# Attention layers: maxima stored by way of a 32x32 block transpose, outputs combined on GpSimd inside attention, loads of a pair head by head

## The chip, the cores and the metric

The kernel runs on one core of one Trainium2 chip. The metric is the device time of one execution in microseconds (us), the median of several runs. Five engines run side by side, each through its own queue in order: TensorE (PE, with its weight loads PEld), VectorE (DVE), ScalarE (ACT), GpSimd (POOL) and SyncE (SP). SP issues all the DMAs of this kernel; an instruction that waits on SP holds back every DMA queued behind it. TensorE's clock is granted by a throttle, and the profile tells its share of full speed.

## The reference

Four layers in a row, A, B, A, B. Each normalizes its input, attends and adds the result to what came in. A is multi-head attention with 32 heads of 18 elements; B has 32 query heads and one shared key and value head.

```python
B, S, D, H = 1, 2048, 576, 32          # Dh = D // H = 18
def _A_ref(x, wqkv, wo):
    qkv = (x @ wqkv).reshape(B, S, 3, H, Dh).transpose(2, 0, 3, 1, 4)
    q, k, v = qkv[0], qkv[1], qkv[2]
    scores = jnp.einsum("bhqd,bhkd->bhqk", q, k) * (Dh ** -0.5)
    p = softmax(scores, axis=-1)
    o = jnp.einsum("bhqk,bhkd->bhqd", p, v)
    return o.transpose(0, 2, 1, 3).reshape(B, S, D) @ wo
# _B_ref: q as above from x @ wq; k = x @ wk and v = x @ wv are one head for all 32
x = A_x
x = x + _A_ref(layernorm(x), A_wqkv, A_wo)
x = x + _B_ref(layernorm(x), B_wq, B_wk, B_wv, B_wo)
x = x + _A_ref(layernorm(x), A_wqkv, A_wo)
x = x + _B_ref(layernorm(x), B_wq, B_wk, B_wv, B_wo)
```

All is float32. Layernorm has no weights.

## The kernel before

A layer has three stages: projection, attention, output projection. They overlap at their ends.

**Projection.** Tokens go in eight tiles of 256. Rows are normalized, transposed and split into a high part (rounded to the float32r type of the matrix unit) and a low part (the rest), and multiplied in three products (high by high, high by low, low by high: `TERMS`). The results, split again, are stored to DRAM in `qk_d`; the values stay in `vbuf`.

**Attention.** Heads go in 16 pairs p; a pair's queries go in four parts u of 512. Each (p, u), called a unit here, is eight steps (`STEPS`), so a layer has 64 units and 512 steps (`ns`). The rows of a pair's queries and keys lie in two of six slots of the tile `big`, the first head on partitions 0 to 63, the second on 64 to 127. They are loaded from `qk_d` by `load_pair` (L410), four loads of 54 rows x 2048 in A (query and key of two heads), two in B (the key is shared and loaded once); each load is 432 KB.

In every step PE does four score matmuls to find the maxima (`max_mm`, L432, DVE reduces each 1024 columns at L438), four score matmuls for the exponential (`exp_mm`, L549, ACT takes the exponential at L552 into `pt`), and the products of `pt` with the values (`pv_block`, L566) into the bank `oacc`. The maxima run `LEAD` = 14 steps ahead of the exponentials: after a unit's last maximum, `max_final` reduces on DVE (L527, `mm`), negates and splits on POOL (L529 to L532, `hl`), `max_store` (L536) writes the 128 x 16 values to `m_d` in DRAM, transposing them element by element on the way, and `max_rows` (L540) loads them back as two further rows of the queries in `big`, two DMAs, one for each head. The key has ones there, so that the second score matmul subtracts the maximum. `exp_mm` of the unit cannot begin before these rows are in `big`.

A unit's output in `oacc` (128 x 512) has, for each of the two heads, two partial sums at partitions 64a and 64a + 32: 18 rows of outputs and one of the softmax's sum. ACT copies it to SBUF (L572, `oc`). Then, each at its step after the unit's end: `o_out` issues four loads that spread the sums over partitions (`lt`, L586) and four stores of the outputs (L590) to `o_d[0]` and `o_d[1]`; `l_sum` adds the two sums on POOL (L594); `l_inv` inverts on DVE (L598); `l_out` stores the inverses to `r_d` (L601); `l_spread` copies them, repeated over 18 rows, from DRAM to DRAM into `o_d[2]` (L607). The order of all this is written out by hand: `at(step, function)` puts a function into the list of a step, and each step runs its list and then its matmuls. So the order on every queue follows the step numbers, while each engine goes on as soon as what it waits for is there. The constants `NM_AT`, `ROW_AT`, `O_AT` and so on are those steps.

The weights of the output projection and of the next layer are loaded and split into high and low on POOL during attention (`load_w`, L121 and L143).

**Output projection.** For each of eight token tiles of 256, `out_rows` (L235, L237) loads three tensors: the two partial outputs and the inverses. `out_t` adds the partial outputs (POOL, L244 and L248), multiplies by the inverses (DVE, L245 and L249) and splits into high (ACT, L119, or DVE, L121) and low (DVE, L247 and L251). `out_w` (L258) multiplies each chunk of 128 tokens in two halves with the weights (`natural`, L198), adds the residual rows (L263) and stores them (L264). The next layer's first rows are loaded and normalized meanwhile.

Of the kernel before, what the change touches and what calls it, by code (L numbers as in the profile page):

```python
# [38 lines left out]

STEPS = 8
LEAD = 14
NM_AT = 2
ROW_AT = 4
O_AT = 4
SUM_AT = 7
INV_AT = 9
R_AT = 10
SPREAD_AT = 12  # L50


FIRST_A = 6
# [2 lines left out]
AHEAD_B = 3  # L56

OUT_AHEAD = 2  # L60
TAIL = 2


@with_exitstack
def tile_kernel(ctx: ExitStack, tc: tile.TileContext, A_x, A_wqkv, A_wo, B_x, B_wq, B_wk, B_wv, B_wo, out):
# [31 lines left out]


    m_d = [dram.tile([2, 2, 4, P], F32, name=f"m_d{i}") for i in range(4)]
    o_d = dram.tile([3, D, S], F32, name="o_d")  # L100
    r_d = dram.tile([H, S], F32, name="r_d")
    x_d = [dram.tile([S, D], F32, name=f"x_d{i}") for i in range(2)]


# [12 lines left out]
    def copy(eng, dst, src):  # L117
        if eng is nc.scalar:
            eng.activation(dst, src, AF.Copy)  # L119
        else:  # L120
            eng.tensor_scalar(dst, src, 1.0, 0.0, op0=OP.mult, op1=OP.add)  # L121
# [107 lines left out]

    def out_rows(tt):  # L230
        ts = slice(tt * 256, tt * 256 + 256)
        o4 = [pool.tile([P, 4, 256], F32, tag="o4", bufs=4, name="o4") for _ in range(3)]
        o1 = pool.tile([P, 3, 256], F32, tag="o1", bufs=2, name="o1")
        for i in range(3):
            nc.sync.dma_start(o4[i], o_d[i, :512, ts].rearrange("(c p) t -> p c t", p=P))  # L235
        for r in (0, 64):
            nc.sync.dma_start(o1[r:r + 64], o_d[:, 512:, ts].rearrange("i p t -> p i t"))  # L237
        ors[tt] = o4, o1

    def out_t(tt, hi):  # L240
        (a, b, r), l = ors.pop(tt)
        ot = ots_[tt] = pool.tile([P, 9, 256], F32R, tag="xt", name="ot")
        ot_f = ot.bitcast(F32)
        nc.gpsimd.tensor_tensor(a, a, b, op=OP.add)  # L244
        nc.vector.tensor_tensor(a, a, r, op=OP.mult)  # L245
        copy(hi, ot[:, 0:4], a)
        nc.vector.tensor_tensor(ot[:, 5:9], a, ot_f[:, 0:4], op=OP.subtract)  # L247
        nc.gpsimd.tensor_tensor(l[:, 0], l[:, 0], l[:, 1], op=OP.add)  # L248
        nc.vector.tensor_tensor(l[:, 0], l[:, 0], l[:, 2], op=OP.mult)  # L249
        copy(hi, ot[:, 4], l[:, 0])  # L250
        nc.vector.tensor_tensor(ot[64:, 4], l[64:, 0], ot_f[64:, 4], op=OP.subtract)  # L251
# [6 lines left out]
    def out_w(c, x_new_prev):  # L258
        xr = xrs.pop(c)
        ot = ots_[c // 2][:, :, c % 2 * P:(c % 2 + 1) * P]  # L260
        for h in range(2):
            cs = slice(h * 288, (h + 1) * 288)
            nc.vector.tensor_tensor(xr[:, cs], natural(ot, h, mtile), xr[:, cs], op=OP.add)  # L263
        nc.sync.dma_start(x_new_prev[c * P:(c + 1) * P, :], xr)  # L264

    ors, ots_, lts, rls = {}, {}, {}, {}
    xhs, xts = {}, {}

    def trans(c):
        tt, u = divmod(c, 2)  # L270
        if u == 0:
            xts[tt] = pool.tile([P, 9, 256], F32R, tag="xt", name="xt")
        xh = xhs.pop(c)
        split_rows(xts[tt][:, :, u * P:(u + 1) * P], *transposed(xh, xh[:, 512:640]))

# [12 lines left out]

    def out_proj(x_res_prev, x_new_prev):

        for c in range(3):
            load_res(c, x_res_prev)
        yield -1
        for c in range(NCH):
            out_w(c, x_new_prev)
            load_res(c + 3, x_res_prev)
            if c >= OUT_AHEAD:
                run_tail(TAIL)
            tt = c // 2
            if c % 2 == 0 and 1 <= tt < 7:  # L300
                out_t(tt + 1, nc.scalar)
            if c % 2 == 1 and tt < 6:
                out_rows(tt + 2)
            yield c
        assert not tail and not ors


    load_x(0, x_in)
    for layer in range(4):
# [83 lines left out]
        def load_rows(slot, c0, step, t0, t1):  # L393

            for a in range(2):
                c = c0 + a * step
                nc.sync.dma_start(big_f[64 * a:64 * a + 3 * DH, slot, t0:t1],
                                  qk_d[c:c + DH, :, t0:t1].rearrange("c i t -> (c i) t"))
# [8 lines left out]
                fixed_rows(q_slot(p), False)  # L407
            load_rows(q_slot(p), 2 * p * DH, DH, t0, t1)

        def load_pair(p):  # L410
            load_q(p)
            if is_a:
                load_k(p)

        mxs, nms, pts, ocs = {}, {}, {}, {}

# [108 lines left out]
        def max_final(p, u):  # L525
            mm = pool.tile([P, 8], F32, name="mm")
            nc.vector.reduce_max(mm, mxs.pop((p, u)), axis=AX.X)  # L527
            neg = pool.tile([P, 8], F32, name="neg")
            nc.gpsimd.tensor_scalar(neg, mm, -1.0, 0.0, op0=OP.mult, op1=OP.add)  # L529
            hl = pool.tile([P, 2, 8], F32R, name="hl")  # L530
            copy(nc.gpsimd, hl[:, 0], neg)
            nc.gpsimd.tensor_tensor(hl[:, 1], neg, hl.bitcast(F32)[:, 0], op=OP.subtract)  # L532
            nms[p, u] = hl.bitcast(F32)

        def max_store(p, u):
            nc.sync.dma_start(m_d[u].rearrange("j a q p -> p (j a q)"), nms.pop((p, u)).rearrange("p j b -> p (j b)"))  # L536

        def max_rows(p, u):
            for a in range(2):
# [37 lines left out]
            if 0 <= n < ns and (half or n % STEPS):  # L577
                pv_block(n, half if n % STEPS else None)

        def o_out(p, u):  # L580
            oc = ocs.pop((p, u))
            lt = lts[p, u] = pool.tile([P, 2, 8], F32, name="lt")
            for a in range(2):
                for i in range(2):
                    r = 64 * a + 32 * i + DH
                    nc.sync.dma_start(lt[64 * a:64 * a + 64, i, :], oc[r:r + 1, :])  # L586
            for a in range(2):
                for i in range(2):
                    r, c = 64 * a + 32 * i, (2 * p + a) * DH
                    nc.sync.dma_start(o_d[i, c:c + DH, u * 512:(u + 1) * 512], oc[r:r + DH, :])  # L590

        def l_sum(p, u):
            lt = lts[p, u]
            nc.gpsimd.tensor_tensor(lt[:, 0], lt[:, 0], lt[:, 1], op=OP.add)  # L594

        def l_inv(p, u):
            rl = rls[p, u] = pool.tile([P, 8], F32, name="rl")
            nc.vector.reciprocal(rl, lts.pop((p, u))[:, 0])  # L598

        def l_out(p, u):  # L600
            nc.sync.dma_start(r_d[2 * p:2 * p + 2, u * 512:(u + 1) * 512].rearrange("a (t e) -> a t e", e=8),  # L601
                              rls.pop((p, u)))

        def l_spread(p, u):
            us = slice(u * 512, (u + 1) * 512)
            for h in (2 * p, 2 * p + 1):
                nc.sync.dma_start(o_d[2, h * DH:(h + 1) * DH, us], r_d[h:h + 1, us].to_broadcast([DH, 512]))  # L607

        todo = {}

# [4 lines left out]
        for p in range(NPAIR):  # L615
            for u in range(4):
                b = STEPS * (4 * p + u) + STEPS - 1
                at(b + NM_AT, max_store, p, u)
                at(b + ROW_AT, max_rows, p, u)
                for d, f in ((O_AT, o_out), (SUM_AT, l_sum), (INV_AT, l_inv), (R_AT, l_out), (SPREAD_AT, l_spread)):  # L620
                    at(b + LEAD + d, f, p, u)
            if p + 1 < NPAIR:
                b = LEAD + 32 * (p - 2) + 32
                at(b if p >= 2 else max(b, LEAD + 2 + 16 * p), load_pair, p + 1)
        for c in range(5):
            at(49 + 4 * c, finish_loads)
            at(48 + 4 * c, load_wsm, c, A_wo if is_a else B_wo, nc.gpsimd, nc.gpsimd, True)
# [6 lines left out]
                at(b + 2, load, c, (0,), nc.gpsimd, nc.gpsimd, True)  # L634

        b = LEAD + ns
        at(b - 10, out_rows, 0)
        at(b - 7, out_t, 0, nc.vector)
        at(b - 6, out_rows, 1)
        at(b - 3, out_t, 1, nc.vector)  # L640
# [4 lines left out]
        for st in range(done // 4, ns + LEAD + O_AT + 1):  # L645
            se = st - LEAD
            for f, args in todo.pop(st, []):
                f(*args)
            for i in range(4):
                if 0 <= se < ns:  # L650
                    exp_mm(*divmod(se // STEPS, 4), se % STEPS * 4 + i, st >= ns)
                if done < st * 4 + i + 1 <= ns * 4:
                    max_mm(*divmod(st // STEPS, 4), st % STEPS * 4 + i)
                left = 2 * -se - i // 2
                if i == 1:
                    pv_slot(se - 2, 1)
                elif i == 3:
                    pv_slot(se - 1, 0)
                if se < 0 and i % 2 and len(fill) * every >= left and (left % every == 0 or len(fill) >= left):
                    f, args = fill.pop(0)  # L660
                    f(*args)
            if se == ns - 1:
                tail = [todo.pop(n, []) for n in range(ns + LEAD + O_AT + 1, ns + LEAD + SPREAD_AT)]
# [37 lines left out]
```

## Time and profile before

| | us |
|---|---|
| median of 3 runs | 7502.77 (7489.41 to 7513.87) |
| the profiled execution's own time | 7491.71 |
| its span, first to last instruction | 7489.9 |
| PE busy | 6380.8 (85%) |
| DVE busy | 5458.4 (73%) |
| ACT busy | 4720.5 (63%) |
| POOL busy | 521.3 (7%) |

The mean granted clock is 0.912. A profile line of the waits reads: who waited, for what, how many us in all, how many times, the longest. A line of the groups reads: line, engine, operation, what is written and read, shapes, count; then busy us, the mean of one in ns; then the idle time of the engine just before, and what ended it. A timeline line reads: start in us, duration, engine, line, operation, how many in a row. SPq is SP's queue issuing a DMA; its duration is that of the issue, not of the transfer.

### The profile page before, as it was taken

Reading aid. Unit: us, or ns where it says so; the run is one execution under the profiler, and the core shown is the slowest. Engines: PE = TensorE matmul, PEld = TensorE weight load, DVE = VectorE, ACT = ScalarE, POOL = GpSimd, SP = SyncE. Lnnn points to the kernel's source line nnn. Section 1 sums busy time; section 2 is a strip of 40 time slices with the busy share of each in tenths; the row PEclk is TensorE's granted clock in tenths of the full one; section 3 lists DMA queues with packets and bytes.
Section 4 is the critical chain, followed back from the end, with each engine's and each line's share of the span. In section 5 each row is a group of like instructions: output and inputs, shape, how many; then the busy total and the mean of one; then the engine's idle time right before and its main releaser. Section 6 shows DMA issues by size and latency. Waiting matters only on the chain.

```text
span 7489.9 us, 132853 instructions
## 1 busy us (share of the span) xinstructions
PE 6380.8 (85%) x53280; PEld 2788.6 (37%) x53280; DVE 5458.4 (73%) x5480; ACT 4720.5 (63%) x8896; POOL 521.3 (7%) x1479
## 2 busy tenths in 40 slices
PE   9888888888788888889698888888887888888897
PEld 9332222233633333333493322222336333333334
DVE  3787777776478888888337877777864788888883
ACT  2576766676157777777325767666761577777773
POOL 1000000001100000000210000000011000000001
PEclk9899989899889999999898999998998899999998
DMA  5311111112621111111552111111125211111104
GB/s 183 70 35 22 29 29 30 30 21 52 196 48 25 21 21 21 21 21 21 151 163 68 36 21 30 29 30 30 22 60 188 48 25 21 21 21 21 21 12 141
DMA packets 910355, 385.49 MB, mean 51 GB/s; under 512 B 679865, under 2 KB 845041, under 8 KB 900017
## 3 DMA queue, kind: packets, MB, share of 16 engines
q1 hardware_dynamic: 909736, 377.01, 21.6%
q8 instruction: 418, 6.85, 0.4%
q14 instruction: 201, 1.64, 0.1%
HBM read 226.22 MB, written 164.46 MB: 52 GB/s over the span
## 4 chain that ended last, share of the span: by engine, by line
DMA 42%; PE 31%; SPq 11%; ACT 7%; issue 5%; DVE 3%; POOL 1%; ACTq 0%; POOLq 0%; DVEq 0%
DMA m_d<-hl 31%; PE pse L549 13%; PE oacc L566 10%; SPq L586 6%; DMA big<-m_d 5%; ACT pt L552 5%; SPq L590 4%; PE psq L327 4%; PE psn L198 2%; DMA o<-o_d 2%; PE psm L432 2%; ACT oc L572 2%; DMA r_d<-rl 1%; DVE mx L438 1%; POOL o L244 1%
## 5 line engine op out<-in xcount | busy, mean ns | idle before, releaser
L438 DVE TENSOR_REDUCE mx<-psm 128x1 f32<-128x1024 f32 x4096 | 4980.2, 1223 | 1254.1 <-PE psm L432 1064.6
L552 ACT ACTIVATE pt<-pse 128x512 f32<-128x512 f32 x8192 | 4415.9, 600 | 1740.8 <-PE psm L432 1233.9
L549 PE MATMUL pse<-big 64*128 64x512 f32 x8192 | 3180.5, 467 | 812.6 <-DMA big<-m_d 703.6
L432 PE MATMUL psm<-big 62*128 62x512 f32 x8192 | 3228.5, 472 | 52.5 <-DVE mx L438 42.7
L566 PE MATMUL oacc<-pt,vbuf 128*19 128x256 f32 (+1 forms) x30720 | 2653.0, 419 | 0.0
L549 PEld LDWEIGHTS pse<-big 64*128 64x128 f32 x8192 | 1305.2, 195 | 2818.3 <-ACT pt L552 1937.6
L432 PEld LDWEIGHTS psm<-big 62*128 62x128 f32 x8192 | 1301.1, 196 | 155.6 <-DVE mx L438 131.7
L566 PEld LDWEIGHTS oacc<-pt,vbuf 128*19 128x19 f32 x30720 | 529.8, 98 | 1451.3 <-issue 1445.2
L198 PE MATMUL psn<-wsm,ot 128*128 128x288 f32 x1792 | 296.9, 335 | 203.4 <-DVE xr L263 203.4
L327 PE MATMUL psq<-xt,big 128*128 128x256 f32 (+1 forms) x3136 | 422.0, 295 | 25.3 <-DVE ev L337 16.2
L327 PEld LDWEIGHTS psq<-xt,big 128*128 128x128 f32 (+1 forms) x3136 | 402.5, 198 | 41.6 <-DVE ev L337 19.2
L529 POOL TENSOR_SCALAR neg<-mm 128x8 f32<-128x8 f32 x256 | 50.4, 197 | 4834.8 <-DVE mm L527 4728.4
L198 PEld LDWEIGHTS psn<-wsm,ot 128*128 128x128 f32 x1792 | 289.7, 226 | 211.7 <-issue 210.0
L331 ACT ACTIVATE ev<-psq 128x512 fp32r<-128x512 f32 (+2 forms) x148 | 73.1, 494 | 434.7 <-PE psq L327 409.6
L119 ACT ACTIVATE ot<-o 128x1024 fp32r<-128x1024 f32 (+1 forms) x48 | 35.3, 736 | 402.3 <-DVE o L245 362.7
L337 DVE TENSOR_TENSOR ev<-psq,ev 128x512 fp32r<-128x512 f32 (+2 forms) x120 | 69.7, 592 | 197.6 <-ACT ev L331 187.2
L245 DVE TENSOR_TENSOR o<-o,o 128x1024 f32<-128x1024 f32 x32 | 42.2, 1320 | 222.9 <-POOL o L244 114.4
L263 DVE TENSOR_TENSOR xr<-psn,xr 128x288 f32<-128x288 f32 x128 | 56.3, 455 | 183.8 <-PE psn L198 183.0
L572 ACT ACTIVATE oc<-oacc 128x512 f32<-128x512 f32 x256 | 154.5, 604 | 34.9 <-PE oacc L566 34.3
L198 PE MATMUL psn<-wsm,xt 128*128 128x288 f32 x896 | 125.0, 295 | 0.0
L198 PEld LDWEIGHTS psn<-wsm,xt 128*128 128x128 f32 x896 | 120.1, 188 | 2.9 <-issue 1.5
L594 POOL TENSOR_TENSOR lt<-lt 128x8 f32<-128x8 f32 x256 | 53.0, 207 | 822.9 <-DMA lt<-oc 822.3
(52 smaller groups left out, 1004.5 us busy)
## 6 DMA issues: line engine op xcount, KB each, us to landing
big<-qk_d SPq DMA_DIRECT2D x180, 432.0 KB
qk_d<-ev SPq DMA_DIRECT2D x192, 256.0 KB
o<-o_d SPq DMA_DIRECT2D x96, 512.0 KB
o_d<-oc SPq DMA_DIRECT2D x1024, 36.0 KB
qk_d<-ev SPq DMA_DIRECT2D x240, 128.0 KB
o_d<-r_d SPq DMA_DIRECT2D x512, 36.0 KB
lt<-oc SPq DMA_DIRECT2D x1024, 2.0 KB
x_d<-xr SPq DMA_DIRECT2D x48, 288.0 KB
```

The lines of the kernel that those rows point to most:

```text
L198: nc.tensor.matmul(ps, lhs[:, xc, :], wsm[:, wc, h * 288:(h + 1) * 288], start=i == 0, stop=i == len(TERMS) - 1)
L244: nc.gpsimd.tensor_tensor(a, a, b, op=OP.add)
L327: nc.tensor.matmul(ps[:n, k, :], w[:, wc, :n], xt[:, xc, :], start=j == 0, stop=j == len(TERMS) - 1)
L331: nc.scalar.activation(ev[0][:n, :g], ps[:n, :g], AF.Copy)
L432: nc.tensor.matmul(ps[:, i % 2], q[b:b + KM, c0:c0 + P], k[b:b + KM, kb * 512:(kb + 1) * 512], start=True, stop=True)
L438: nc.vector.reduce_max(mxs[p, u][:, a * 4 + qc, j // 8:j // 8 + 1], ps.rearrange("p a t -> p (a t)"), axis=AX.X)
L549: nc.tensor.matmul(e, k[r:r + KE, kc * P:(kc + 1) * P], q[r:r + KE, u * 512:(u + 1) * 512], start=True, stop=True)
L552: nc.scalar.activation(pt, e, AF.Exp, scale=SCALE)
L566: nc.tensor.matmul(oacc[j:j + DH + 1, cs], v[:, kc, 2 * p + a if is_a else 0, :], pts[p, u, i][:, cs], start=kc < 2, stop=kc >= 14 and hal ...
L572: nc.scalar.activation(oc, oacc, AF.Copy)
L586: nc.sync.dma_start(lt[64 * a:64 * a + 64, i, :], oc[r:r + 1, :])
L590: nc.sync.dma_start(o_d[i, c:c + DH, u * 512:(u + 1) * 512], oc[r:r + DH, :])
```

## The change

Four things change together.

- **The maxima's store.** `hl` is one of two fixed tiles of 128 x 32, filled with zeros once at the start. `max_store` transposes it on DVE by blocks of 32 x 32 and issues four stores, one for each block of 32 partitions, each of 16 rows of 32 elements. `max_rows` stands one step later (`ROW_AT` 5 for 4).
- **The outputs.** `o_sum` copies the second partial of each head to the partitions of the first and adds, on POOL; so the two sums are added in the same step as the outputs. `l_part` spreads the two sums with two loads; `l_inv` and `l_out` are as before; `l_rows` loads the inverses, repeated over 18 rows, into SBUF (`rbs`); `o_mul` multiplies and splits on POOL; `o_out` stores the high and low part, four DMAs.
- **The output projection** loads the high and low part as they are; `out_t` is gone. Three buffers of `xt` instead of two hold them. The store of a chunk is issued after the work of the next, and a residual load two chunks ahead instead of three.
- **The pair's loads** are issued one by one, one every eight steps (every four for the second pair), instead of all in one step.

```diff
-ROW_AT = 4
-O_AT = 4
-SUM_AT = 7
-INV_AT = 9
-R_AT = 10
-SPREAD_AT = 12
+ROW_AT = 5
+SUM_AT = 3
+L_AT = 4
+INV_AT = 7
+R_AT = 7
+RB_AT = 9
+MUL_AT = 11
+O_AT = 13
...
+    rbs = [cst.tile([P, 512], F32, name=f"rb{i}") for i in range(2)]
+    sums = [cst.tile([P, 512], F32, name=f"os{i}") for i in range(2)]
+    hls = [cst.tile([P, 32], F32R, name=f"hl{i}") for i in range(2)]
+    for t in rbs + sums + [h_.bitcast(F32) for h_ in hls]:
+        nc.gpsimd.memset(t, 0.0)
...
     def out_rows(tt):
...
+        for i in range(2):
+            nc.sync.dma_start(ot[:, 5 * i:5 * i + 4], o_d[i, :512, ts].rearrange("(c p) t -> p c t", p=P))
+            nc.sync.dma_start(ot[64 * i:64 * i + 64, 4], o_d[i, 512:, ts])
-    def out_t(tt, hi):
...
+        def load_part(p, i):
+            if i < 2:
+                if i == 0 and p < 3:
+                    fixed_rows(q_slot(p), False)
+                load_rows(q_slot(p), 2 * p * DH, DH, 0, S, (i,))
+            else:
+                if i == 2 and p < 3:
+                    fixed_rows(k_slot(p), True)
+                load_rows(k_slot(p), D + 2 * p * DH, DH, 0, S, (i - 2,))
...
         def max_store(p, u):
-            nc.sync.dma_start(m_d[u].rearrange("j a q p -> p (j a q)"), nms.pop((p, u)).rearrange("p j b -> p (j b)"))
+            tr = pool.tile([P, 32], F32, name="tr")
+            nc.vector.transpose(tr, nms.pop((p, u)).bitcast(F32))
+            for b in range(4):
+                nc.sync.dma_start(m_d[u].rearrange("j a q (b i) -> b (j a q) i", b=4)[b], tr[32 * b:32 * b + 16, :])
...
+        def o_sum(p, u):
+            oc = ocs.pop((p, u))
+            t = sums[u % 2]
+            for j in (0, 64):
+                copy(nc.gpsimd, t[j:j + 32], oc[j + 32:j + 64])
+            nc.gpsimd.tensor_tensor(t[:96], t[:96], oc[:96], op=OP.add)
+        def l_part(p, u):
+            lt = lts[p, u] = pool.tile([P, 8], F32, name="lt")
             for a in range(2):
+                nc.sync.dma_start(lt[64 * a:64 * a + 64, :], sums[u % 2][64 * a + DH:64 * a + DH + 1, :])
...
+        def l_rows(p, u):
+            for a in range(2):
+                nc.sync.dma_start(rbs[u % 2][64 * a:64 * a + DH, :],
+                                  r_d[2 * p + a:2 * p + a + 1, u * 512:(u + 1) * 512].to_broadcast([DH, 512]))
+        def o_mul(p, u):
+            t = sums[u % 2]
+            nc.gpsimd.tensor_tensor(t[:96], t[:96], rbs[u % 2][:96], op=OP.mult)
+            hi, lo = his[p, u] = [pool.tile([P, 512], F32R, tag="oh", name="oh") for _ in range(2)]
+            copy(nc.gpsimd, hi[:96], t[:96])
+            nc.gpsimd.tensor_tensor(lo[:96], t[:96], hi.bitcast(F32)[:96], op=OP.subtract)
+        def o_out(p, u):
+            for i, t in enumerate(his.pop((p, u))):
+                for a in range(2):
+                    c = (2 * p + a) * DH
+                    nc.sync.dma_start(o_d[i, c:c + DH, u * 512:(u + 1) * 512], t.bitcast(F32)[64 * a:64 * a + DH, :])
...
             if p + 1 < NPAIR:
-                b = LEAD + 32 * (p - 2) + 32
-                at(b if p >= 2 else max(b, LEAD + 2 + 16 * p), load_pair, p + 1)
+                for i in range(4 if is_a else 2):
+                    at(LEAD + 32 * (p - 1) + 1 + 8 * i if p else LEAD + 1 + 4 * i, load_part, p + 1, i)
```

In the order of SP's queue a unit's DMAs now are: two loads `lt` (waiting for POOL's add), four stores of the next maxima (waiting for the transpose), four stores of outputs, the store of the inverses (waiting for the reciprocal), the two rows of the maxima, two loads `rb` (waiting for the store of the inverses), one load of a pair. On POOL, after the maxima's `hl` come multiply, copy and subtract of the unit before, then two copies and the add. On DVE the transpose stands behind two reduces of the next unit, the reciprocal behind six more.

More of the change, by code (lines that the diff above doesn't have):

```diff
@@ L61 @@
 TAIL = 2
+XT = 3
 @with_exitstack
@@ L231, in out_rows @@
         ts = slice(tt * 256, tt * 256 + 256)
[L232 to L238, printed above, removed]
-    def out_t(tt, hi):
[L241 to L251, printed above, removed]
+        ots_[tt] = pool.tile([P, 9, 256], F32R, tag="xt", bufs=XT, name="ot")
+        ot = ots_[tt].bitcast(F32)
+        for i in range(2):
+            nc.sync.dma_start(ot[:, 5 * i:5 * i + 4], o_d[i, :512, ts].rearrange("(c p) t -> p c t", p=P))
+            nc.sync.dma_start(ot[64 * i:64 * i + 64, 4], o_d[i, 512:, ts])
     def load_res(c, src):
@@ L636, in tile_kernel @@
         b = LEAD + ns
[L637 to L640, printed above, removed]
+        for i in range(XT - 1):
+            at(b - 8 + 2 * i + 4 * (i // 2), out_rows, i)
         for _ in range(FIRST_A if is_a else 0):
```

79 lines of the change are left out of this document (29 added, 50 removed).

## The prediction

> **What bounds the kernel now.** I read the page's chain first, then the waits (the engines', then SyncE's own), then the timeline of single units, then the groups kept apart by shape. A unit is one (p, u): one pair of heads, 512 queries, eight steps.
>
> ```profile
> DMA 42%; PE 31%; SPq 11%; ACT 7%; issue 5%; DVE 3%; POOL 1%; ACTq 0%; POOLq 0%; DVEq 0%
> PE pse L549 <- DMA big<-m_d: 703.6, 224, 13.1
> SPq L540 <- DMA m_d<-hl: 2540.9, 241, 11.5
> SPq L607 <- DMA r_d<-rl: 730.2, 225, 13.1
> ```
>
> The chain says DMA, though a DMA engine is mostly idle in attention. PE stands 704 us, in 224 of the 256 units, until the maxima's rows are in `big`; SP spends 2541 us on the store they come from, some 10.5 us each time. The store writes 128 x 16 separate 4-byte elements, 2048 packets.
>
> ```profile
> 734.15 0.40 SPq L536 DMA_DIRECT2D m_d<-hl  x1
> 745.33 0.54 SPq L540 DMA_DIRECT2D big<-m_d  x2
> 745.96 1.35 SPq L397 DMA_DIRECT2D big<-qk_d  x4
> 747.41 0.59 SPq L601 DMA_DIRECT2D r_d<-rl  x1
> 760.22 1.48 SPq L607 DMA_DIRECT2D o_d<-r_d  x2
> ...
> 765.96 0.40 SPq L536 DMA_DIRECT2D m_d<-hl  x1
> 777.23 0.53 SPq L540 DMA_DIRECT2D big<-m_d  x2
> ```
>
> SP's timeline in layer 0. From L536 to L540 passes the store, 11.2 us each time. At 745.96 four loads of 432 KB enter; the small `r_d` store behind them is waited for until 760.22, 12.8 us instead of the usual 2.3, and everything queued behind L607 is late, the next maxima's store too (32 us after the last, instead of 22 to 24). So A layers pay twice: a small stall in each unit, one of 10 us in every fourth.
>
> From first to last L536 in the four layers pass 1602.5, 1494.3, 1593.6 and 1496.0 us (starts 221.4 to 1823.9, 2092.6 to 3586.9, 3967.7 to 5561.3, 5835.4 to 7331.4): 6186 us for 252 units, 24.55 each. Where PE does not wait, VectorE paces:
>
> ```profile
> L438 DVE TENSOR_REDUCE mx<-psm x4096: 1171/1225/1227, 196.3 to 7327.3; 128x1 f32<-128x1024 f32 x196
> L598 DVE RECIPROCAL rl<-lt 128x8 f32<-128x8 f32 x256 | 49.5, 193 | 33.8 <-POOL lt L594 33.7
> L244 POOL TENSOR_TENSOR o<-o,o 128x1024 f32<-128x1024 f32 x32 | 75.7, 2364 | 280.0 <-DMA o<-o_d 280.0
> L143 POOL TENSOR_TENSOR wsm<-raw,wsm 128x288 fp32r<-128x288 f32 x48 | 38.7, 807 | 4.0
> L121 POOL TENSOR_SCALAR wsm<-raw 128x288 fp32r<-128x288 f32 x60 | 26.3, 438 | 125.9 <-DMA raw<-in_A_wo_dram 65.1 <-DMA raw<-in_B_wo_dram 56.6 <-DMA raw<-in_A_wqkv_dram 3.6
> ```
>
> Sixteen reduces back to back are 16 x 1.222 = 19.55 us (runs of nine take 10.99); the step in which `oacc` is evicted adds 0.4 (the final reduce `mm` and a 0.28 us bubble), the reciprocal 0.24. ScalarE needs 32 x 0.6 + 0.6 = 19.8 us, so nothing can go much below 20. A unit with no wait is 20.2 us; the other 4.35 are the wait (704/252 = 2.8) and the slow matmuls behind it (794 ns against 492), some 1.5.
>
> **The change, part by part.** *The maxima's store (L536)* becomes a transpose on DVE and four stores of 16 rows x 128 bytes: 64 packets for 2048. Nearest row: the `r_d` store, 128 packets of 32 bytes, 2.3 us from issue until SP goes on. Bounds 2.0 and 11.3 (no gain at all); I take 2.3, since the packets shrink 32-fold. ROW_AT moves the rows' load one step later.
>
> *The transpose* (128x32) is added to the pacing engine. Rows near it: 0.17 (`mm`), 0.19 (reciprocal), 0.31 (128x64, L226). I take 0.25 plus 0.05 of semaphore, 0.3 per unit; ends 0.2 and 0.4. It waits on `hl` from POOL, ready 0.85 us after `mm`, and stands two reduces (2.6 us) behind it: covered.
>
> *POOL's new work*, in order after `hl`: multiply, copy, subtract for unit n-1, two copies and an add for unit n; the 0.2 us add L594 goes. By shape: two-input ops at 512 elements lie between 0.807 (288) and 2.364 (1024), on the line 1.28; one-input ops on the line from 0.197 (8 elements) to 0.438 (288), 0.63. 3 x 1.28 + 3 x 0.63 + 3 gaps of 0.08 = 6.0 us. No row shows POOL copying to other partitions; two such copies may cost 0.2 or 1.28 each, so 5.1 to 7.3. POOL, 7% busy, has room; what counts is who waits.
>
> SP waits for that add in `l_part`, and the four stores of the maxima are queued behind it. Clock from the end of `mm` (1134.16 here):
>
> ```profile
> 1132.84 2.42 SPq L586 DMA_DIRECT2D lt<-oc  x4
> 1133.99 0.17 DVE L527 TENSOR_REDUCE mm<-mx 128x8 f32<-128x16 f32 x1
> ...
> 1134.81 0.20 POOL L532 TENSOR_TENSOR hl<-neg,hl 128x8 fp32r<-128x8 f32 x1
> ...
> 1136.61 0.20 POOL L594 TENSOR_TENSOR lt<-lt 128x8 f32<-128x8 f32 x1 [1.60 <-DMA lt<-oc]
> 1137.00 0.40 SPq L536 DMA_DIRECT2D m_d<-hl  x1
> ```
>
> `hl` at +0.85, POOL's add done at +6.85, two `lt` loads issued to +8.1 (0.61 each). The row shows 1.97 us from the fourth `lt` issue to its user, so `lt` is there at +9.5. The reciprocal, on DVE after two reduces, transpose and six reduces, would start at +10.2: covered by 0.7 us. If not, DVE itself stands, and the unit lengthens by the difference. The four stores (0.3 each) go out by +9.3 and land by +11.3; behind them four `o_d` stores and the `r_d` store (reciprocal at +10.4) to +11.2; the rows are issued at +11.3 and +11.6 and, by the 1.7 us of now (1126.46 to the exp at 1128.26), land at +13.3. The exps reach them at +14.1 in a clean unit now, +14.4 with the transpose. Covered by about 1 us.
>
> *The pair's loads* come one per unit (2.8 us each: four held `r_d` back 11), behind `l_rows`, some 5 us before the next `mm`: nothing small stands behind them in time. Their 10 us stalls, in the 4.35 above, go. `l_rows` waits 2.3 us for `r_d`; the `rb` loads land near +16, the multiply needs them at +21.
>
> Attention: 252 x (24.55 - 20.5) = **-1021 us** (ends: 20.2 gives -1096; with `lt` late by 1.3, 21.8, -693).
>
> *Weight splits on POOL* (L121, L143) cross the new chain in some 7 units a layer: up to 1 us each, **+30**, ends 0 and 100.
>
> *Output projection*: POOL, DVE and ACT work of `out_t` leaves it (103.6, 123.6 and 35.4 us in all); a token tile loads 1.18 MB for 1.92.
>
> ```profile
> 1940.41 0.82 DVE L263 TENSOR_TENSOR xr<-psn,xr 128x288 f32<-128x288 f32 x2
> ...
> 1956.55 0.82 DVE L263 TENSOR_TENSOR xr<-psn,xr 128x288 f32<-128x288 f32 x2
> ```
>
> A tile (two chunks) takes 16.3 us now: loads, then POOL, DVE, ACT, DVE in turn. PE alone needs 4 x 1.85 = 7.4 (the first chunks, from 1866.10). One set of loads took 8.0 us, 240 GB/s; at that rate the new loads plus 1.18 MB of residual in and out take 9.8. So 6 tiles x 4 layers x 6.5 = -156; the last unit's longer chain (sum, `lt`, `r_d`, `rb`, multiply) holds SP a few us per layer: **-140**, ends -60 and -214.
>
> *Six memsets at the start* on POOL: four at the 1.1 us of L443 before the first `rs`: **+4**, ends 0 and 5.
>
> Sum: 7489.9 - 1021 + 30 - 140 + 4 = 6363; the profiled run's own time is 2 above its span, the median 11 above that: **6370**.
>
> **The rivals.**
> 1. *DVE waits for `lt` at the reciprocal*: the margin is 0.7 us and the cross-partition copies are unpriced. Late by 0.5 to 2 us: 256 x that, 6500 to 6880. For it: the chain POOL, SP, DMA, DVE closes within one unit. Against: oc is evicted before `mm`, so POOL starts at once.
> 2. *The transpose stands behind POOL ops.* In out_t a 0.42 us DVE op with two SBUF inputs (L251) once took 2.62, beside a 2.36 us add on POOL; the transpose runs amid POOL's 1.28 us ops, waiting 0.6 on average: +154, 6525. Against it: it has one SBUF input. The Trainium skill (SBUF — State Buffer, "Who interferes with whom") says that VectorE and GpSimd share a port pair that one holds for a whole instruction, a VectorE op using it only with two SBUF inputs or in a two-port mode, a reduce never. The reduces agree (maximum 1.227 us, with POOL's splits among them); for the transpose no run here shows which it is, so the rule gives 6370 or 6525.
> 3. *The store stays slow*: four small DMAs land as late as one. Units like those without load stalls now, 23.7: -214 - 140, about 7140. Against: the `r_d` row.
> 4. *Slower than before*: POOL's chain at twice its rows or more (POOL spans are rough, and copies across partitions may be slow), so that DVE stands at the reciprocal. Break-even: 4.05 + 140/252 = 4.6 us a unit, a chain of 6.0 + 0.7 + 4.6 = 11.3 us. At 12 us about 7680.
>
> **How the numbers follow.** Forecast as summed (6250 to 6470) 0.56; rival 1 0.20; rival 2 0.10; rival 3 0.07; rival 4 0.06; between, 0.01. The range holds the forecast and rivals 1 and 2: 6240 to 6880. Less than 0.3% is what a measurement cannot tell from no change. Faster 0.93, same 0.01, slower 0.06.
>
> **What would show it.** Right: SP's wait on the maxima's store falls from 10.5 us a unit to below 2; PE's 704 us behind `big<-m_d` nearly go; unit period near 20.5; no DVE idle before the reciprocal; granted clock in attention near 1. Wrong: DVE idle before the reciprocal with `lt` as releaser (rival 1), transposes above 0.5 us (2), SP still standing on `m_d` (3), POOL copies above 2 us (4).

## The result, and the profile after

The changed kernel takes 6313.87 us (median of 4 runs, 6308.48 to 6320.79) where the kernel before took 7499.08 us beside it (7489.41 to 7513.87): a ratio of 0.8419, 95% interval 0.8402 to 0.8435. The forecast was 6370, with 6240 to 6880 as its range. Its profiled execution took 6320.79 us, with a span of 6319.0 and a mean granted clock of 0.979 (0.912 before).

The waits of the engines, then SyncE's own, in the changed kernel (who waited, for what: us in all, times, longest us):

```profile
DVE rl L599 <- DMA lt<-os: 103.5, 30, 17.5
PE pse L553 <- DMA big<-m_d: 74.8, 101, 2.4
...
SPq L595 <- POOL os L590: 2754.0, 230, 16.5
SPq L607 <- DMA r_d<-rl: 209.9, 243, 1.9
SPq L544 <- DMA m_d<-tr: 10.0, 17, 1.6
```

SP's 2541 us at the maxima's store are 10 us now. It stands as long as before, but at another place: at L595, for POOL's sum. PE's 704 us for the rows are 74.8, in 101 units. The first line looks worse than it is: taking the times of the single units, VectorE waits 142 us at the reciprocal (under several releasers), and 108 us of them lie in the last three units of the four layers, where no reduces are left that they could delay.

The groups of the changed kernel, shapes apart (busy us, mean ns, idle before):

```profile
L590 POOL TENSOR_TENSOR os<-os,oc 96x512 f32<-96x512 f32 x256 | 327.8, 1280 | 21.4
L132 POOL TENSOR_SCALAR os<-oc 32x512 f32<-32x512 f32 x512 | 316.0, 617 | 66.2 <-ACT oc L576 28.2
L132 POOL TENSOR_SCALAR oh<-os 96x512 fp32r<-96x512 f32 x256 | 159.7, 624 | 22.4
L538 DVE STREAM_TRANSPOSE tr<-hl 128x32 f32<-128x32 f32 x256 | 51.6, 202 | 5.6 <-POOL hl L533 5.6
```

POOL's prices came out as interpolated: 1.28 us with two inputs, 0.62 with one, the copies across partitions 0.617, no dearer than others. The transpose takes 0.20 us.

One unit of the changed kernel, from four answers of the timeline (POOL, SP, VectorE, PE):

```profile
408.66 0.20 POOL L533 TENSOR_TENSOR hl<-neg,hl 128x8 fp32r<-128x8 f32 x1
413.64 1.28 POOL L590 TENSOR_TENSOR os<-os,oc 96x512 f32<-96x512 f32 x1
...
414.94 1.55 SPq L595 DMA_DIRECT2D lt<-os  x2
416.55 1.97 SPq L540 DMA_DIRECT2D m_d<-tr  x4
...
420.76 0.71 SPq L544 DMA_DIRECT2D big<-m_d  x2
...
407.84 0.17 DVE L528 TENSOR_REDUCE mm<-mx 128x8 f32<-128x16 f32 x1
410.56 0.20 DVE L538 STREAM_TRANSPOSE tr<-hl 128x32 f32<-128x32 f32 x1
417.88 0.19 DVE L599 RECIPROCAL rl<-lt 128x8 f32<-128x8 f32 x1
...
422.66 0.46 PE L553 MATMUL pse<-big 64*128 64x512 f32 x1 [0.55 <-DMA big<-m_d]
```

Counted from the end of `mm` (408.01), `hl` is done at +0.85, POOL's add at +6.91, the transpose at +2.75. The store could leave there, but is issued at +8.54, behind the two `lt` loads that wait for POOL's add. The rows are asked for at +12.75 and PE waits 0.55 us for them. Over the units in the middle of the layers (the 5th to the 55th), the medians are +6.94 for the first `lt` load, +8.13 for the first store and +12.39 for the rows.

Where the 1171 us of the two profiled spans went (attention is the 252 intervals from a layer's first `mm` to its last; the output projection runs from the last value product to the next layer's first product):

| us | before | after | difference | forecast |
|---|---|---|---|---|
| attention | 6185.1 (24.54 a unit) | 5202.0 (20.64 a unit) | -983 | -1021 + 30 |
| output projections | 493.6 | 306.0 | -188 | -140 |
| all else | 811.2 | 811.0 | 0 | +4 |

### The profile page after: what moved, and what is told of

The parts are those of the page before. It is cut to its first block, busy times and chain, and to the rows that moved or that the text cites. A ratio compares the mean times of both kernels' runs of the same rounds, so it can differ in the third digit from the quotient of the medians.

```text
span 6319.0 us, 134168 instructions
## 1 busy us (share of the span) xinstructions
PE 6064.2 (96%) x53280; PEld 2682.3 (42%) x53280; DVE 5323.0 (84%) x5592; ACT 4691.3 (74%) x8848; POOL 1815.4 (29%) x2701
## 4 chain that ended last, share of the span: by engine, by line
PE 55%; DVE 14%; DMA 8%; POOL 7%; ACT 7%; SPq 6%; issue 4%; POOLq 0%; DVEq 0%; ACTq 0%
PE pse L553 23%; PE oacc L570 20%; DVE mx L439 13%; PE psq L322 5%; ACT pt L556 5%; PE psn L209 4%; DMA big<-m_d 3%; PE psm L433 3%; SPq L540 2%; ACT oc L576 2%; SPq L621 1%; POOL oh L615 1%; POOL os L590 1%; POOL os L132 1%; DMA x_d<-xr 1%
## 5 line engine op out<-in xcount | busy, mean ns | idle before, releaser
L433 PE MATMUL psm<-big 62*128 62x512 f32 x8192 | 3065.8, 453 | 48.2 <-DVE mx L439 39.2
L553 PE MATMUL pse<-big 64*128 64x512 f32 x8192 | 3000.0, 446 | 116.4 <-DMA big<-m_d 74.8
L570 PE MATMUL oacc<-pt,vbuf 128*19 128x256 f32 (+1 forms) x30720 | 2534.9, 402 | 0.0
L553 PEld LDWEIGHTS pse<-big 64*128 64x128 f32 x8192 | 1233.6, 185 | 1981.1 <-ACT pt L556 1897.1
L433 PEld LDWEIGHTS psm<-big 62*128 62x128 f32 x8192 | 1232.2, 187 | 150.5 <-DVE mx L439 130.9
L612 POOL TENSOR_TENSOR os<-os,rb 96x512 f32<-96x512 f32 x256 | 327.5, 1279 | 113.2 <-DMA rb<-r_d 101.6
L132 POOL TENSOR_SCALAR os<-oc 32x512 f32<-32x512 f32 x512 | 316.0, 617 | 66.2 <-ACT oc L576 28.2
L615 POOL TENSOR_TENSOR oh<-os,oh 96x512 fp32r<-96x512 f32 x256 | 327.9, 1281 | 21.4
L590 POOL TENSOR_TENSOR os<-os,oc 96x512 f32<-96x512 f32 x256 | 327.8, 1280 | 21.4
L258 DVE TENSOR_TENSOR xr<-psn,xr 128x288 f32<-128x288 f32 x128 | 56.4, 454 | 270.2 <-PE psn L209 124.1
L193 ACT ACTIVATE xt<-ps 128x512 fp32r<-128x512 f32 x64 | 38.2, 596 | 215.7 <-PE ps L201 214.9
```

Of the source, the lines that this page charges most:

```text
L433: nc.tensor.matmul(ps[:, i % 2], q[b:b + KM, c0:c0 + P], k[b:b + KM, kb * 512:(kb + 1) * 512], start=True, stop=True)
L553: nc.tensor.matmul(e, k[r:r + KE, kc * P:(kc + 1) * P], q[r:r + KE, u * 512:(u + 1) * 512], start=True, stop=True)
L570: nc.tensor.matmul(oacc[j:j + DH + 1, cs], v[:, kc, 2 * p + a if is_a else 0, :], pts[p, u, i][:, cs], start=kc < 2, stop=kc >= 14 and hal ...
L590: nc.gpsimd.tensor_tensor(t[:96], t[:96], oc[:96], op=OP.add)
L612: nc.gpsimd.tensor_tensor(t[:96], t[:96], rbs[u % 2][:96], op=OP.mult)
L615: nc.gpsimd.tensor_tensor(lo[:96], t[:96], hi.bitcast(F32)[:96], op=OP.subtract)
```

## The experiments

The same two quantities for every run; the time is the median. The kernel before took 7499 to 7514 us beside the changed kernel and the first eight runs. The last four ran on a chip where it took 7213 to 7216, at a mean granted clock of some 0.925 where the others showed some 0.909; these four are therefore compared by their traces.

| kernel | us | attention, us a unit | four output projections, us |
|---|---|---|---|
| before | 7499 | 24.54 | 494 |
| after | 6314 | 20.64 | 306 |
| store alone | 6455 | 20.52 | 493 |
| loads alone | 7142 | 23.12 | 493 |
| store and loads | 6357 | 20.09 | 500 |
| after, old store | 8753 | 30.18 | 310 |
| after, store first | 6197 | 20.22 | 308 |
| after, store and sum first | 6186 | 20.14 | 320 |
| after, chain +2.8 | 7116 | 23.70 | 318 |
| after, chain +5.5 | 8011 | 27.20 | 329 |
| store first, chain +2.8 | 6902 | 22.86 | 318 |
| store and sum first, chain +2.8 | 6204 | 20.16 | 332 |
| after, loads at once | 6295 | 20.63 | 304 |
| after, two buffers | 6339 | 20.60 | 338 |

### The maxima's store alone

The kernel before, with this and the two zeroed `hl` tiles:

```diff
-            nc.sync.dma_start(m_d[u].rearrange("j a q p -> p (j a q)"), nms.pop((p, u)).rearrange("p j b -> p (j b)"))
+            tr = pool.tile([P, 32], F32, name="tr")
+            nc.vector.transpose(tr, nms.pop((p, u)).bitcast(F32))
+            for b in range(4):
+                nc.sync.dma_start(m_d[u].rearrange("j a q (b i) -> b (j a q) i", b=4)[b], tr[32 * b:32 * b + 16, :])
```

> The kernel before, with only the transpose on VectorE and the four 128-byte-row stores (rows' load still at step 4, pair's loads and output path as before). Theory (the 4-byte store is what paced attention, and the load stalls were only its followers): the store leaves at +2.9 us after the maxima's last reduce and lands at about +5.5, a late r_d (some 10 us in every fourth unit of the A layers) moves it to +8 at most, the exps need it at +14, so units come down to about 20.4 in A and B layers alike: 252 x (24.55 - 20.4) = -1045, 6450 us. Rival (the four-load stall is a cost of its own): B layers 20.4, A layers keep about 9 us in every fourth unit, +270, 6720 us. Rival (POOL's and SP's work of the output path was needed too): above 6900.

6454.71 us, ratio 0.8593 (0.8567 to 0.8618). The store is the bulk of the gain. That the time meets the first theory's 6450 is luck: stalls that it took as covered still cost something, and a unit without them is shorter than its 20.4. B layers come to 20.06 and 20.15 us a unit, A layers stay at 20.83 and 21.04. SP's timeline in an A layer of this run shows what is left:

```profile
1060.53 1.70 SPq L542 DMA_DIRECT2D m_d<-tr  x4
...
1069.82 2.21 SPq L401 DMA_DIRECT2D big<-qk_d  x4
1072.44 0.60 SPq L607 DMA_DIRECT2D r_d<-rl  x1
1082.88 1.47 SPq L613 DMA_DIRECT2D o_d<-r_d  x2
1084.46 2.42 SPq L592 DMA_DIRECT2D lt<-oc  x4
...
1088.61 1.69 SPq L542 DMA_DIRECT2D m_d<-tr  x4
```

`r_d` behind the four loads still takes 10.4 us, and the next store comes 28.1 us after the last instead of 20. Part of that is covered: the unit shown takes 21.4 us, and the longest of the A layers, 24 in all after their first ones, 22 to 27. Both theories were half right, by some 105 us over two layers.

### The loads alone

The kernel before, with `load_pair` split into `load_part`, as in the diff of the change.

> The kernel before, with only the pair's rows loaded head by head. Theory: the 10 us stalls in every fourth unit of the A layers go, A layers come to the B layers' 23.7 us a unit: 1601 + 1592 - 2 x 1494 = -205, 7285 us. Rival (nothing is gained while SP stands at the store in each unit anyway, or single loads now delay r_d in every unit): 7400 to 7500 us.

7141.54 us, ratio 0.9504 (0.949 to 0.9518): 372 us, more than either theory. A layers fall to 23.21 and 23.29 us a unit, below what B layers had been (23.7), and B layers fall too, to 23.12 and 22.88: their two loads of a pair had held `r_d` as well, here for 7.9 us in a B layer of the kernel before:

```profile
2581.11 0.65 SPq L397 DMA_DIRECT2D big<-qk_d  x2
2581.86 0.59 SPq L601 DMA_DIRECT2D r_d<-rl  x1
2589.75 1.52 SPq L607 DMA_DIRECT2D o_d<-r_d  x2
```

The store's price is untouched; SP stands 10.9 us between these two lines of its timeline in the run with the loads alone:

```profile
1011.08 0.39 SPq L542 DMA_DIRECT2D m_d<-hl  x1
1021.98 0.52 SPq L546 DMA_DIRECT2D big<-m_d  x2
```

### Store and loads, with the old output path

> The kernel before, with the transposed store and the loads head by head, the output path as before. Theory (stalls only followed the store): the same as the store alone within 20 us, about 6440; the output path of the change is then worth the rest, 6440 - 6314 = about -126: -188 in the four output projections and +60 in attention (waits for the rows and for lt). Rival (the four-load stall has its own cost): 270 us less than the store alone.

6357.29 us, ratio 0.8462 (0.845 to 0.8475): 97 us below the store alone, more than the first theory's 20 and less than the rival's 270. Alone the two parts gave 1059 and 372 us, together 1156: so 275 us are gained by either part. Attention is 20.09 us a unit, 0.55 shorter than in the whole change. So the output path of the change wins 194 us in the projections and loses 139 in attention. SP's and VectorE's timeline in this run:

```profile
1007.10 1.69 SPq L548 DMA_DIRECT2D m_d<-tr  x4
1009.83 0.53 SPq L552 DMA_DIRECT2D big<-m_d  x2
...
1003.82 0.17 DVE L537 TENSOR_REDUCE mm<-mx 128x8 f32<-128x16 f32 x1
1003.90 1.21 DVE L448 TENSOR_REDUCE mx<-psm 128x1 f32<-128x1024 f32 x1
1005.41 1.23 DVE L448 TENSOR_REDUCE mx<-psm 128x1 f32<-128x1024 f32 x1 [0.29 <-PE psm L442]
1006.55 0.20 DVE L546 STREAM_TRANSPOSE tr<-hl 128x32 f32<-128x32 f32 x1
1006.68 12.19 DVE L448 TENSOR_REDUCE mx<-psm 128x1 f32<-128x1024 f32 x10
```

From the first of the four stores until the rows go out pass 2.7 us; the 4-byte store needed 10.9. The transpose begins while the reduce before it still shows as running, and the next reduce starts 0.13 us after it. The two reduces around it start 1.27 us apart (1005.41 and 1006.68), where 1.22 is usual: 0.05 us is its price on the engine, not its 0.20.

### The old store in the changed kernel

```diff
-            tr = pool.tile([P, 32], F32, name="tr")
-            nc.vector.transpose(tr, nms.pop((p, u)).bitcast(F32))
-            for b in range(4):
-                nc.sync.dma_start(m_d[u].rearrange("j a q (b i) -> b (j a q) i", b=4)[b], tr[32 * b:32 * b + 16, :])
+            nc.sync.dma_start(m_d[u].rearrange("j a q p -> p (j a q)"), nms.pop((p, u)).bitcast(F32)[:, 0:16])
```

> The changed kernel with the 4-byte store put back (no transpose, one store of 2048 elements), at its place behind POOL's add and the lt loads. Theory: the store leaves at +8.5 us after the maxima's last reduce, lands 11.2 later at +19.7, the rows at +21.5, where the exps would start at +14.4: PE stands 7 us in each unit and about 1 us of slow matmuls follows, 28 us a unit: 6314 + 252 x 7.6 = 8230 us (7900 to 8500), slower than the kernel before. Rival 3's figure (a slow store in the changed kernel costs what it cost before): 7140 us.

8752.86 us, ratio 1.1653 (1.1635 to 1.1671). The mechanism holds, and the changed kernel without its store is far slower than the kernel before, since the store stands behind POOL's sum. The size is beyond the range given: PE waits 1852 us for the rows (7.35 a unit, the 7 expected), but a unit grows by 9.5. PE's timeline of this run, and its windows (us, busy us of PE, PEld, DVE, ACT and POOL with their counts, then granted clock, DMA share, GB/s):

```profile
1022.12 0.76 PE L550 MATMUL pse<-big 64*128 64x512 f32 x1 [8.45 <-DMA big<-m_d]
1028.28 0.50 PE L550 MATMUL pse<-big 64*128 64x512 f32 x1
```

```profile
1010.00:1013.60 3.60, 3.60 (x37) 1.23 (x36) 3.60 (x4) 3.19 (x7) 0.00 (x0) 1.00 0.75 30
1022.10:1028.20 6.10, 6.08 (x36) 1.99 (x36) 2.96 (x3) 3.15 (x6) 0.00 (x0) 0.52 0.32 85
1028.20:1031.00 2.80, 2.70 (x22) 1.00 (x18) 2.53 (x4) 2.67 (x6) 0.26 (x2) 1.00 0.00 0
```

After the wait the granted clock is 0.52 for 6.1 us, and 36 matmuls go through at half pace; VectorE stands 0.95, 0.92 and 0.16 us between its reduces. These 2.0 us are about what the wait costs on top of itself (9.5 less 7.35).

### The store ahead of the sum's loads

The changed kernel with one order turned round: in the step that holds both, `max_store` comes ahead of `l_part`.

```diff
-            for f, args in todo.pop(st, []):
+            for f, args in sorted(todo.pop(st, []), key=lambda e: e[0] is not max_store):
```

> The changed kernel with one order turned round: in the step that holds both, the maxima's transpose and four stores are written ahead of the two lt loads, so that SP no longer holds them back until POOL's add (+6.9 us after the last reduce). Theory (the changed kernel's attention of 20.64 us a unit against 20.09 in the run of store and loads with the old output path is the rows coming late, 74.8 us of PE's wait in 101 units and the slow matmuls behind it): the store leaves at +3, the rows are there some 4 us before the exps, PE's wait on m_d goes, units at 20.2 to 20.3: -90, 6225 us. Rival (the loss is VectorE's wait for lt at the reciprocal, or POOL's load on shared memory): within 20 us of 6314.

6196.99 us, ratio 0.8253 (0.8236 to 0.827): 117 us from an order on one queue. SyncE's waits of this run:

```profile
SPq L540 <- DVE tr L538: 2258.5, 252, 15.7
SPq L595 <- POOL os L590: 511.3, 226, 4.0
```

SP now stands for the transpose first, the store leaves at +2.8 us after `mm` (+8.1 in the changed kernel, medians), and PE's wait for the rows falls from 74.8 to 0.4 us. The theory holds; 75 of the 106 us that attention gains here are that wait, the rest is not told apart.

### The sum ahead of scaling and splitting

```diff
-MUL_AT = 11
+MUL_AT = 12
```

on top of the last edit.

> As the run with the store first, and POOL's three operations of scaling and splitting (unit n-1) come one step later, behind the two copies and the add of unit n, so that the sum is ready 3.2 us sooner. Theory: VectorE's waits of 0.3 to 2 us at the reciprocal in some 20 units, and those of 5 us where POOL still has weight splits, go too: another -30, units at 20.1 as in the run of store and loads, 6314 - 252 x 0.55 = 6180 us (6165 to 6200). Rival (these waits are covered by something else): the same as the run with the store first.

6186.42 us, ratio 0.8237 (0.8217 to 0.8258), the lowest time of the study. The sum is ready at +3.6 instead of +6.9, and of the 20 units in mid-layer in which VectorE had stood over 0.3 us at the reciprocal in the changed kernel none is left. The waits beside the weight splits, which the theory expected to go as well, stay in the A layers: 5.4 and 4.2 us. Attention gains 21 us of the 30 expected, the projections lose 12, so the time falls by 11 only, and the two intervals overlap: from the times alone the two kernels cannot be told apart.

### POOL's chain made longer

The changed kernel, with the pair of copies made three times (first run) and five times (second); the repeats write the same values again:

```diff
-            for j in (0, 64):
+            for j in (0, 64) * 3:
                 copy(nc.gpsimd, t[j:j + 32], oc[j + 32:j + 64])
```

> The changed kernel with POOL's pair of copies made three times (four more of 0.617 us, 2.5 us more of the chain; the values do not change). Theory (lt is covered by 0.5 us, the rows already late by some 0.3): VectorE stands 2.0 us at the reciprocal in each unit, the rows come another 0.5 late and slow matmuls follow: 2.5 to 3 us a unit, 6950 to 7080 us. Rival (the prediction's margins, 0.7 and 1 us): 1.8 us a unit, 6770. Rival (the chain is not on the path): 6314 within 30.

> The same with the pair of copies made five times (eight more, 4.9 us; a chain of about 10.9 us). The prediction's fourth rival put the break-even with the kernel before at a chain of 11.3 us, which gives some 7400 us here. Theory (each us past the margin costs one, and the wait is long enough for slow matmuls behind it): 4.9 to 6 us a unit, 7570 to 7850 us, slower than before.

7115.94 us (ratio 0.9479, 0.9459 to 0.95) and 8010.71 us (1.067, 1.0648 to 1.0692): both above the ranges given. A repeated copy costs 0.69 with its gap, so the add ends at +9.70 and +12.46 instead of +6.92 (medians): 2.78 and 5.54 us more. VectorE stands 2.29 and 4.95 us at the reciprocal in a mid-layer unit, 0.5 to 0.6 less than was added: that is the margin. But a unit grows by 3.06 and 6.56. The windows of the first of the two runs (columns as above) show the difference:

```profile
1006.00:1010.50 4.50, 4.50 (x47) 1.51 (x45) 2.62 (x3) 3.71 (x8) 2.18 (x3) 1.00 0.02 4
1010.50:1012.70 2.20, 0.50 (x5) 0.18 (x1) 1.29 (x3) 1.03 (x2) 0.00 (x0) 1.00 0.05 4
1012.70:1014.50 1.80, 1.75 (x11) 0.45 (x11) 1.80 (x2) 0.60 (x1) 0.00 (x0) 0.63 0.35 83
1014.50:1016.60 2.10, 2.10 (x16) 0.66 (x12) 1.20 (x2) 1.09 (x2) 0.00 (x0) 0.51 0.05 6
1016.60:1020.00 3.40, 3.40 (x37) 1.30 (x36) 3.02 (x4) 2.53 (x5) 0.00 (x0) 1.00 0.48 137
```

VectorE's wait stops PE through the full `psm` banks; PE is nearly idle for 2.2 us (it stands 1.76 us without a matmul) and pays with 3.9 us at a clock of 0.51 to 0.63. So each us that VectorE stands costs 1.3 us a unit (3.06 for 2.29, 6.56 for 4.95). In the first run late rows are part of it: PE waits 179.5 us for them, where it was 74.8. In the second it waits 35.0, and the price is the same: the rows do not make it. By the added chain, with the margin in it, it is 1.14 us a unit between the changed kernel and the first run (802 / 2.78 / 252), and 1.28 between the two runs. On that last line the kernel before (7504 beside them) is reached with the add at +10.9, a chain of 10.05 us after `hl`.

### The same, with the rows off the chain, and with the sum first

> The kernel with the store first, and POOL's pair of copies made three times. In the changed kernel this lengthening (2.8 us with its gaps) cost 802 us, with both lt and the rows late. Here the rows are off the chain, so only VectorE's wait at the reciprocal is left. Theory (the reciprocal's wait carries most of it, and slow matmuls follow it): VectorE stands 2.2 to 2.8 us a unit, 6197 + 252 x (2.3 to 2.9) = 6780 to 6930 us. Rival (the late rows carried it): 6197 to 6300.

> The kernel with store and sum first, and the same lengthening. Theory (what counts is the time from the last reduce to the sum, not POOL's work): the sum is ready at +3.7 + 2.8 = +6.5, still ahead of the changed kernel's +6.9, so VectorE waits as it does in the run with the store first or less: 6186 to 6210 us. Rival (POOL's busy time itself slows VectorE or the transfers): 6250 and more.

6902.44 and 6204.34 us, both within the theories' ranges. With the store first, attention grows from 20.22 to 22.86 us a unit, 2.64 of the 3.06 above, and the waits of this run leave one cause:

```profile
DVE rl L599 <- DMA lt<-os: 706.9, 252, 17.8
...
PE pse L553 <- DMA big<-m_d: 8.2, 7, 2.1
```

So the reciprocal's wait carries most of it, the late rows at most the rest (the two kernels ran on different chips). With store and sum first the same 2.8 us cost nothing: 20.16 us a unit against 20.14. What counts is the time from `mm` to the sum, not POOL's work; POOL is no bound. Here the add ends at +6.39.

### The loads at once

The changed kernel with `load_pair` of before in place of `load_part`.

> The changed kernel with a pair's four loads (two in B) put back into one burst, behind the rb loads. With the new store alone the loads head by head were worth 97 us. Theory (a burst now holds lt rather than r_d: it ends some 9 us after the last reduce, and lt is issued at +7): VectorE stands 2 to 4 us in one unit of four of the A layers, 30 x 3 = +90, and 0 to 20 in B: 6380 to 6430 us. Rival (fully covered): 6314 within 15.

6295.36 us. The theory fell. Attention is 20.63 us a unit, as with the loads one by one. SP's timeline in an A layer of this run:

```profile
1055.92 1.35 SPq L392 DMA_DIRECT2D big<-qk_d  x4
1068.34 1.13 SPq L589 DMA_DIRECT2D lt<-os  x2
```

The burst goes out 12.4 us before the next small DMA, longer than four loads of 2.8 us. So in the whole change it is the burst's place behind the `rb` loads that covers it, and splitting it is worth nothing there.

### Two buffers for the projection

```diff
-XT = 3
+XT = 2
```

> The changed kernel with two buffers instead of three for the split outputs (XT = 2), so that one token tile is loaded ahead of the projection instead of two. In the changed kernel the first ten half-tiles run at TensorE's 1.85 us each; in the kernel before, a gap of 17.6 us lay after the fourth chunk of 128 tokens. Theory (the part of the projection's gain that the prediction did not count is that start, some 12 us a layer, and it hangs on the third buffer): the projection is 76.5 us a layer now and 87 to 92 with two buffers, the attention stays: 6314 + 4 x (10 to 16) = 6355 to 6380 us. Rival (the gain is all in the smaller tile cost): 6314 within 15.

6339.01 us. The projections take 338 us, 84.6 a layer, 8 more than with three buffers; less than expected. PE's timeline in the first projection, first in the changed kernel, then in this run:

```profile
1565.76 18.84 PE L209 MATMUL psn<-wsm,ot 128*128 128x288 f32 x140
1587.30 9.22 PE L209 MATMUL psn<-wsm,ot 128*128 128x288 f32 x56 [2.70 <-DVE xr L258]
```

```profile
1576.22 11.40 PE L209 MATMUL psn<-wsm,ot 128*128 128x288 f32 x84
1593.01 2.26 PE L209 MATMUL psn<-wsm,ot 128*128 128x288 f32 x8 [5.39 <-DMA ot<-o_d]
```

PE runs 140 products in a row where it now runs 84, then stands 5.4 us for its tile. By the additions of the residual (L258; L263 before) the fifth chunk comes 12.8 us after the fourth here and 3.7 with three buffers; in the kernel before the gap lay between the third and the fourth and was 17.6 us. There VectorE has `out_t` of the third tile in front of the addition and waits for POOL's part of it, and this stands in POOL's queue behind the `l_sum` of one of the last units, whose sums came late:

```profile
1880.99 0.20 POOL L594 TENSOR_TENSOR lt<-lt 128x8 f32<-128x8 f32 x1 [26.95 <-DMA lt<-oc]
1883.52 1.73 DVE L245 TENSOR_TENSOR o<-o,o 128x1024 f32<-128x1024 f32 x1 [11.40 <-POOL o L244]
1889.53 9.02 PE L198 MATMUL psn<-wsm,ot 128*128 128x288 f32 x56 [14.19 <-DVE xr L263]
```

POOL's addition L244 begins at 1881.15, right behind L594. How long it would have waited for the loads of its own tile, issued from 1869.29 on, is not shown.

## Why the prediction was right, and where it was not

**What bounds the kernel: right.** The store of 4-byte elements paced attention. Given alone, the new store brings 1059 us of the 1185. Four of the five signs named came: SP's wait on it 0.04 us a unit, PE's 704 us down to 74.8, a unit of 20.64 (forecast 20.5), a granted clock of 0.99 in the attention stages. The fifth, no idle time of VectorE before the reciprocal, did not: it stands there over 0.3 us in 20 units in mid-layer, and 5 us beside the weight splits. Rival 3, the store as slow as before, is out.

**The unit: right in sum, by luck, since two errors cancel.** Without a wait it is 19.94 us (median of the store-and-loads run), not 20.5. Two reduces start 1.22 us apart; with an instruction of 0.2 us between them it is 1.35 (`mm`), 1.27 (transpose) and 1.25 (reciprocal), medians of that run. So they cost 0.12, 0.05 and 0.03 us, because the next starts before the last one's shown end; the sum had taken the full durations and 0.05 for a semaphore on top. In the other direction 0.7 us a unit of waits, and of what follows them, stayed.

**"Covered by about 1 us" for the rows: wrong.** This step failed. The term that was too small is SP's issuing. By the medians the `lt` loads began as forecast and took 1.13 us for 1.22, but the four stores took 1.97 us to issue, 0.49 each, not 0.3; the output stores and `r_d` behind them ended 2.14 us later, not 1.9. So the rows went out at +12.39 (+12.75 in the unit shown), not at +11.3, and PE waited in 101 units. SP's own wait for the store to land is 10 us in all, so it was the issuing that made them late. Putting the store first gave 117 us. The text had seen that SP's wait for POOL's add holds the stores; it priced the margin instead of asking what the order cost.

**The reciprocal's margin of 0.7 us: nearly right.** It is 0.5 to 0.6. POOL's chain was 6.07 us (forecast 6.0), its add at +6.92 (forecast +6.85). Rival 1 stayed at some 20 units in mid-layer.

**Rival 2: out.** 248 of the 256 transposes started while POOL was busy, and none took more than 0.213 us. By the Trainium skill (SBUF — State Buffer, "Who interferes with whom") an instruction of VectorE with one SBUF input, outside the two-port modes, does not meet POOL; the trace agrees.

**Rival 4's break-even of 11.3 us: too late.** It lies at a chain of some 10.05 us. The rival counted each us of VectorE's wait once, and the runs paid 1.3. That PE's slow clock after the wait is what was missing fits the windows, and in the longest chain no wait for the rows explains it; it was not tried apart. The kernel with that chain, 11.6 us, took 8011 us where the rival's line gives about 7580.

**The loads one by one: the mechanism right, the place wrong.** The stalls of the A layers went, and in the kernel before the split is worth 372 us alone. In the whole change it is worth nothing, because a burst behind `l_rows` meets no small DMA. "Units like those without load stalls now, 23.7" was not such a unit: B layers had load stalls too, and without them it is 23.1.

**The output projection: the term was too small, -140 for -188.** A token tile takes 10.65 us (from the fifth chunk on, first layer: 58.6 us for 5.5 tiles) where 9.8 was forecast. But the sum counted six tiles only and left out the start: between the third and the fourth chunk of the kernel before 17.6 us pass, in which VectorE waits for POOL and does `out_t` of the third tile, and in the changed kernel the first five chunks come 3.7 to 4.5 us apart. With two buffers one gap of 12.8 is back, so the start hangs on the third buffer too.

**The splits on POOL and the memsets.** Two neighbouring long units near the end of each A layer, 23.1 and 29.0 us in the first, 25.7 and 26.7 in the third, lie where the next layer's weights are split. They account for about 24 of the 30 us; that POOL's splits made them is argued from SP's 204 us of wait on those operations at L595 and was not tried. The memsets do not show: the first `mm` starts 1.9 us later, and all else is equal to 0.2 us.

**Small slips in the working.** 6363 + 2 + 11 is 6376, not 6370; the two lines shown for a token tile lie 16.1 us apart, not 16.3; from 1126.46 to 1128.26 it is 1.8 us, not 1.7. No argument hangs on them.

## What to carry to other kernels

Write small values to DRAM in rows, not in elements: a block transpose that costs the pacing engine 0.05 us turned 10.9 us of store into 2.7. When a long chain is moved onto an idle engine, look at the queue that waits for its end, and put what is already finished ahead of that wait; here one order was worth 117 us, a tenth of the whole change. A margin of less than a microsecond should be counted with the issue time of every DMA in front of it.

## What the runs showed of the hardware

- A wait of PE costs more than itself. After 8.45 us without work the granted clock was 0.52 for 6.1 us; after 2.2 us with little work (1.76 us without a matmul) it was 0.51 to 0.63 for 3.9 us; after 0.55 us nothing changed (a granted clock of 1.00 from 422 to 426 us in the changed kernel). The Trainium skill (TensorE: Matmul & The Clock Gate, "What's actually happening") halves the clock after an idle window of about 3.4 us; the first case agrees, the second came after a shorter gap, and there the measurement decides.
- The kernel before, full of such waits, took 7213 to 7216 us on one chip, at a granted clock of some 0.925, and 7499 to 7514 on the others, at some 0.909. Whether the waits cost less on that chip is not shown: no other kernel was run on both.
- The issue of one DMA on SP took, by medians of the changed kernel, 0.26 us (a row load of the maxima), 0.27 (a 432 KB load), 0.42 (a store of the maxima) and 0.57 (an `lt` load). The four stores of a unit's maxima take 1.97 us in a row there and 1.69 in the run of store and loads.
